# Decode attention with an MLP: four heads of wo moved to the end of the load stream, the final section inside the TensorE loop, wider value and weight products, and q with x stationary

## Chip, cores, metric

One core of a Trainium2 chip (trn2) runs the kernel. The metric is the device time of one execution in microseconds. Runs of this one-core program mostly agreed within 0.5% on one chip; a ratio is taken against runs of the kernel before on the same chip, in the same rounds.

## The reference

```python
x = A_x                                   # (4, 1, 448): four sequences, one token each
xn = layernorm(x)
q  = (xn @ wq)                            # 16 heads of 256; 8 K/V heads, so 2 q heads share one
s  = softmax(q k^T / 16) v  @ wo          # k, v caches: (4, 8, 8192, 256) bf16, 268 MB together
h  = layernorm(xn) @ w3; b = xn + gelu(h) @ w4      # at sequence length 1 the shift branch is zero
out = x + s * silu(b)
```

268 of the 279 MB read are K and V cache, and every byte is used once. There are 32 "heads" in the kernel's loop: 4 sequences times 8 K/V heads, each 4 MB of K and 4 MB of V.

## The kernel before

One DMA queue, issued by SyncE, carries all loads in one order. K and V have two buffers each; a load waits until its buffer is free, which for K is when the last transpose of the head before the last was copied out.

```python
# prog_sp: the load stream
wq -> vb[1];  w3, w4 -> vb[0];  load_k(0);  load_k(1)
wo (all 16 heads, one transfer)
for h in range(2, NH):
    load_k(h)            # waits for v_k >= h-1
    load_v(h - 2)        # waits for v_v
load_v(NH - 2)
load_v(NH - 1)           # the last V in four pieces: 2, 1, 0.5, 0.5 MB
```

TensorE transposes K in 128 by 128 blocks (DVE and ScalarE copy them out), forms scores, multiplies p by V two heads later, and at the end multiplies by wo.

```python
# prog_pe
... q product:   112 matmuls, wq stationary (128x128), xnT moving (8 columns)
... w3 product:  49 matmuls;   w4 product: 56 matmuls, 112 columns each, in four column groups
take(pe, "v_bout")
with nc.Fori(0, NH // 2, head_slot={PE: 0}):      # two heads a pass
    body(0); body(1)
h = NH - 1                                         # the final section follows the loop
f_bc(h); f_tr(h - 2); f_o(0..4); f_sum(h); f_pv(h - 1); f_o(5); f_tr(h - 1); f_o(6)
for i in range(4):                                 # the four V pieces of the last head
    take(pe, "dvl%d" % i, 16)
    ... 128 matmuls in all, V stationary
take(pe, "v_ot"); f_o(7)                           # 16 wo matmuls after the last V piece
# cut: body(h): 16 x (8 transposes, 8 score matmuls), and 64 value matmuls of 256 columns
```

## Time and profile before

| | before |
|---|---|
| time, median of three (range) | 661.82 us (660.87 to 663.16) |
| span of the profiled run | 658.7 us |
| read from HBM | 278.99 MB; 432 GB/s in the middle |
| one 4 MB load | 9.71 us of stream; a head needs two, 19.4 us |
| TensorE, one head, data ready, granted clock 1.00 | 14.13 us |
| last landing; out_b ready | 654.15 us; 656.59 us |

Three things have to be read here. The first is that the stream is the bound: one head takes TensorE 14.13 us and the stream 19.4.

The second is the start. Timeline of the kernel before, TensorE and SyncE (start us, us, engine, line, operation, out<-in, count, and in brackets how long the engine had been idle and what ended that):

```profile
21.77 1.48 PE L515 MATMUL pst<-vb,hT 128*4 128x112 bf16 x56 [1.88 <-PEq L219]
30.96 1.86 PE L528 MATMUL pst<-ident_b,kn 128*128 128x128 bf16 x16 [7.72 <-PEq L219]
...
43.85 0.33 SPq L183 DMA_DIRECT2D kn<-in_A_k_cache_dram  x1
64.95 0.33 SPq L183 DMA_DIRECT2D kn<-in_A_k_cache_dram  x1
...
82.61 0.33 SPq L183 DMA_DIRECT2D kn<-in_A_k_cache_dram  x1
```

The w4 product (L515) ends at 23.3 us; the K transposes (L528) begin at 30.96, as K of head 0 has landed (30.83). TensorE has 7 us in hand. K of head 2 is issued at 43.85 us. At that time wq, w3, w4, K 0 and K 1 are loaded and wo (3.67 MB) is still coming, until 50.23 us. So wo is what bridges the time until TensorE has freed the first K buffer. The stream by stretches of 2 us (each line: stretch, its length, busy us and count of PE, PEld, DVE, ACT, POOL, then the granted TensorE clock, the DMA share and GB/s) does not stop at these places:

```profile
44.00:46.00 2.00, 0.18 (x8) 0.05 (x2) 0.48 (x1) 0.00 (x0) 0.00 (x0) 0.87 1.03 379
46.00:48.00 2.00, 2.00 (x38) 0.94 (x38) 0.00 (x0) 0.00 (x0) 0.00 (x0) 0.50 1.27 479
86.00:88.00 2.00, 1.95 (x35) 1.79 (x32) 1.68 (x5) 1.02 (x1) 0.19 (x1) 1.00 0.99 426
88.00:90.00 2.00, 2.00 (x49) 2.00 (x47) 1.19 (x4) 1.65 (x6) 0.00 (x0) 1.00 1.03 442
```

The third is the tail. Timeline of the kernel before, then its DMA view from 640 to 649 us:

```profile
654.29 0.59 PE L630 MATMUL pst<-pT,kn 128*128 128x32 bf16 x16 [0.62 <-PEq L219]
655.03 0.23 DVE L472 TENSOR_TENSOR OT<-pst,rz 128x2 bf16<-128x2 f32 x2 [6.84 <-DVEq L219]
655.40 0.55 PE L610 MATMUL pst<-wo_sb,OT 128*4 128x112 bf16 x16 [0.53 <-PEq L219]
656.00 0.28 DVE L476 TENSOR_TENSOR res<-pst,sg 128x112 f32<-128x112 f32 x1 [0.74 <-PE pst L610]
656.31 0.28 DVE L478 TENSOR_TENSOR out_b<-res,x 128x112 bf16<-128x112 f32 x1
```

```profile
DMA packets 357, 3.58 MB, mean 398 GB/s; under 512 B 43, under 2 KB 43, under 8 KB 101
q1 hardware_dynamic: 356, 3.56, 94.2%
q8 instruction: 1, 0.02, 0.7%
```

After the last V piece 2.44 us pass until out_b is ready: value matmuls, a DVE product, 16 wo matmuls, two DVE operations. And one packet of the DMA view is no data: 16 KB of instructions (started at 644.15 us, 1.07 us long; another at 651.46).

What that packet does is seen in the landings. Every load has 16 landings in the trace, as many as the page counts DMA engines, so each is read here as one engine's. How far each of the 16 landed behind the first (us), in the kernel before:

| load | first, us | the sixteen, behind the first |
|---|---|---|
| V of head 30 | 640.39 | 0.00 0.14 0.68 0.75 0.76 0.77 1.12 1.22 1.62 1.63 1.69 1.74 1.84 1.93 2.15 **2.37** |
| V of head 31, piece 0 | 645.29 | 0.00 0.14 0.68 0.73 0.74 0.77 1.10 1.20 1.60 1.63 1.68 1.73 1.84 1.93 2.15 **3.96** |
| piece 3 | 650.31 | 0.00 0.14 0.68 0.69 0.75 0.77 1.08 1.18 1.54 1.64 1.68 1.74 1.79 1.88 2.09 **3.84** |

Fifteen engines keep their distance to a hundredth or so. One falls back by 1.6 us between 640 and 649 us, where the instruction packet lies, and never makes it up. The kernel waits for all sixteen (the value matmuls of the last piece start at 654.29, behind the last landing at 654.15), so there, where the slowest engine is 1.75 us behind the fifteenth in place of 0.23, this is about 1.5 us at the end of the kernel.

### The profile page before, as it was taken

The page shows a single profiled execution, that of the slowest core. Times are in us where ns is not written, and L with a number is a line of the kernel's source. Part 1 is how long each engine was busy: PE and PEld are TensorE (multiplying, and loading weights), DVE is VectorE, ACT ScalarE, POOL GpSimd, SP SyncE. Part 2 cuts the span into 40 slices and gives each one's busy share as a digit, 9 for nine tenths or more (in the row PEclk, how much of TensorE's full clock was granted, in tenths as well). Part 3 has the DMA queues.
Part 4 walks back from the last instruction along what each step waited for, and adds up shares of the span by engine and source line. Part 5 has one row for each costly group of instructions (what it writes and reads, how often), then busy time and mean ns, then how long its engine had stood idle before and what let it go on. Part 6 is the DMA issues. An engine that isn't in the chain of part 4 may idle for free. (4 is left out here: it accounts for less than half of the span.)

```text
span 658.7 us, 25245 instructions
## 1 busy us (share of the span) xinstructions
PE 531.3 (81%) x11091; PEld 481.5 (73%) x11091; DVE 260.7 (40%) x585; ACT 252.6 (38%) x362; POOL 17.0 (3%) x76
## 2 busy tenths in 40 slices
PE   1489999896979879678887867987969698867895
PEld 1378888885969778577777756877858688866784
DVE  7234455242433424343433434442524343433440
ACT  1044444451434435234443423443524344423340
POOL 4000000000000000000000000000000000000000
PEclk9988799696797969798987979896979896978996
DMA  8999999999999999999999999999999999999995
GB/s 363 433 410 427 427 432 430 434 434 430 432 432 430 432 434 430 434 432 434 428 434 428 432 432 436 430 432 436 426 434 430 436 430 434 434 426 436 426 426 223
DMA packets 12324, 279.18 MB, mean 424 GB/s; under 512 B 1172, under 2 KB 3224, under 8 KB 3736
## 3 DMA queue, kind: packets, MB, share of 16 engines
q1 hardware_dynamic: 12288, 278.99, 98.9%
q8 instruction: 10, 0.16, 0.1%
q14 instruction: 2, 0.02, 0.0%
q10 hardware_dynamic: 24, 0.01, 0.0%
HBM read 278.99 MB, written 0.00 MB: 424 GB/s over the span
## 5 line engine op out<-in xcount | busy, mean ns | idle before, releaser
L528 PE MATMUL pst<-ident_b,kn 128*128 128x128 bf16 x4096 | 345.5, 238 | 101.2 <-PEq L219 99.7
L265 ACT ACTIVATE kT<-pst 128x1024 bf16<-128x1024 bf16 x224 | 229.4, 1024 | 361.7 <-ACTq L219 361.1
L528 PEld LDWEIGHTS pst<-ident_b,kn 128*128 128x128 bf16 x4096 | 277.6, 108 | 106.4 <-issue 105.8
L263 DVE COPY kT<-pst 128x1024 bf16<-128x1024 bf16 x288 | 197.8, 692 | 282.5 <-DVEq L219 282.3
L540 PE MATMUL psc<-qc,kT 128*128 128x2 bf16 x4096 | 179.2, 165 | 0.7 <-issue 0.7
L540 PEld LDWEIGHTS psc<-qc,kT 128*128 128x128 bf16 x4096 | 158.8, 98 | 22.8 <-issue 22.8
L566 PE MATMUL psv<-vb,pT 128*2 128x256 bf16 x2112 | 84.8, 284 | 2.5 <-issue 1.8
L566 PEld LDWEIGHTS psv<-vb,pT 128*2 128x2 bf16 x2112 | 39.8, 84 | 10.9 <-issue 2.8
L407 DVE TENSOR_REDUCE rmax<-psc 128x2 f32<-128x128 f32 x32 | 9.3, 292 | 49.4 <-DVEq L219 49.4
L576 PE MATMUL psv<-sel,po 128*128 128x2 f32 x136 | 25.1, 289 | 0.7 <-PEq L219 0.6
L576 PEld LDWEIGHTS psv<-sel,po 128*128 128x128 f32 x136 | 23.0, 237 | 0.9 <-issue 0.9
L284 ACT ACTIVATE pT<-psc,negb 128x64 bf16<-128x64 f32 x66 | 20.6, 332 | 5.2 <-ACTq L219 5.2
L412 DVE TENSOR_REDUCE gmax<-psm 2x1 f32<-2x128 f32 x32 | 8.9, 279 | 33.9 <-DVEq L219 33.9
L250 POOL COPY qc<-qT 128x4 bf16<-128x4 bf16 x32 | 5.9, 187 | 584.1 <-DVEq L430 574.5
L552 PEld LDWEIGHTS psm<-diag,ones_f 2*128 2x128 f32 x66 | 12.7, 239 | 6.0 <-issue 4.6
L552 PE MATMUL psm<-diag,ones_f 2*128 2x2 f32 x66 | 15.4, 301 | 1.1 <-PEq L219 0.9
L431 DVE COPY po<-psv 128x256 f32<-128x256 f32 x33 | 14.0, 425 | 4.8 <-DVEq L219 4.1
L284 ACT ACTIVATION_READ_ACCUMULATOR pT<-psc,negb 128x1 f32 x66 | 13.6, 206 | 0.0
L557 PE MATMUL psm<-rowsum,ones_f 128*128 128x2 f32 x66 | 12.4, 257 | 0.0
L486 PE MATMUL pst<-ident_b,xn_b 4*128 4x4 bf16 x14 | 0.6, 161 | 13.5 <-DVE xn_b L333 8.8
L486 PEld LDWEIGHTS pst<-ident_b,xn_b 4*128 4x128 bf16 x14 | 0.5, 100 | 13.6 <-POOL ident_f L243 8.8
L557 PEld LDWEIGHTS psm<-rowsum,ones_f 128*128 128x128 f32 x66 | 10.3, 196 | 0.2 <-issue 0.2
(77 smaller groups left out, 97.1 us busy)
## 6 DMA issues: line engine op xcount, KB each, us to landing
kn<-in_A_k_cache_dram SPq DMA_DIRECT2D x32, 4096.0 KB, 26.0
vb<-in_A_v_cache_dram SPq DMA_DIRECT2D x31, 4096.0 KB, 31.7
vb<-in_A_wq_dram SPq DMA_DIRECT2D x1, 3584.0 KB, 11.3
wo_sb<-in_A_wo_dram SPq DMA_DIRECT2D x1, 3584.0 KB, 46.9
vb<-in_B_w_dram SPq DMA_DIRECT2D x2, 1568.0 KB, 16.3
kn<-in_A_v_cache_dram SPq DMA_DIRECT2D x1, 2048.0 KB, 27.1
kn<-in_A_v_cache_dram SPq DMA_DIRECT2D x1, 1024.0 KB, 29.1
kn<-in_A_v_cache_dram SPq DMA_DIRECT2D x2, 512.0 KB, 30.2
```

Of the source, the lines that this page charges most:

```text
L263: engine.tensor_copy(dst, src).then_inc(S["v_ev"], 1)
L265: engine.activation(dst, src, ACT.Copy).then_inc(S["a_ev"], 1)
L284: ins = act.activation(pv_p[:, :, hh], sc[:, :, hh], ACT.Exp, bias=negb[:, s, hh:hh + 1], scale=SCALE, accum_out=rowsum[:, s, hh:hh + 1])
L407: v.tensor_reduce(rmax[:, :], psc[h % 2][:, 0:NCH * REP].rearrange("p (k h) -> p h k", h=REP), AX.X, ALU.max).then_inc(S["v_rmax"], 1)
L412: v.tensor_reduce(gmax[:, :], psm[0:REP, 0:P], AX.X, ALU.max).then_inc(S["v_s"], 1)
L431: v.tensor_copy(po[:, :], psv[:, 0:DH]).then_inc(S["v_po"], 1)
L528: ins = pe.transpose(dst[:, t * P:(t + 1) * P], kn[:, h % 2, GC * j + kl, half * P:(half + 1) * P], ident_b[:, :])
L540: ins = pe.matmul(psc[h % 2][:, kk * REP:(kk + 1) * REP], kT[:, j % RING, t * P:(t + 1) * P], qc[:, h % 2, half, :], start=(half == 0), st ...
L552: pe.matmul(psm[:, P:P + REP], ones_f[0:REP, :], diag[:, :], start=True, stop=True).then_inc(S["p_m2"], 1)
L557: pe.matmul(psm[:, P + REP:P + 2 * REP], ones_f[:, :], rowsum[:, h % 2, :], start=True, stop=True).then_inc(S["p_m3"], 1)
L566: ins = pe.matmul(psv[o:o + REP, 0:DH], pT[:, h % 2, kk * REP:(kk + 1) * REP], vb[:, h % 2, kk, :], start=(kk < NCG), stop=(kk >= NCH - NCG))
L576: ins = pe.matmul(psv[:, o:o + REP], po[:, dh:DH:NHALF], sel[:, :], start=True, stop=True)
```

## The change

Its intent: load the last four heads' worth of wo behind the last V, so that little work is left after the last landing; keep instruction fetches out of the tail; make TensorE's code shorter. In parts:

1. wo is loaded in two portions: heads 4 to 15 early, heads 0 to 3 in three transfers at the very end.
2. The final section moves into the TensorE loop, under a condition, as a seventeenth pass.
3. Value matmuls take two K/V chunks at once (512 columns, half as many), and the turned sums, which fold the partial sums and bring d to the partitions, therefore take two tiles (four fp32 matmuls for two).
4. The q product has xn stationary (28 matmuls of 512 columns, then four transposes); the w4 product is 14 matmuls of 448 columns in place of 56 of 112, and its follow-up on DVE changes.
5. GpSimd makes the identities first; heads are taken from the last sequence to the first.

```diff
@@ prog_sp
-            sp.dma_start(wo_sb (all heads), A_wo ...).then_inc(S["dwo"], 16)
+            load_wo(NLATE, HQ, "dwo")
...
             load_v(NH - 1)
+            for i, hs in enumerate(LATE):                 # ((0, 1), (2,), (3,))
+                load_wo(hs[0], hs[-1] + 1, "dwl%d" % i)
@@ prog_pe, ahead of the loop
-            for c in range(NQC):
-                for j in range(DK):
-                    ins = pe.matmul(qo[:, g, hh, dh], wq_sb[:, j, c * P:(c + 1) * P], xnT[:, j], ...)
+            pe.wait_ge(S["g_c"], NPC)
+            for j in range(DK):
+                for i in range(NQD):
+                    ins = pe.matmul(q_ps[i * PQ:i * PQ + NHF * Bn, 0:QW], xnT[:, j] ..., 
+                                    wq_sb[:, j, i * QW:(i + 1) * QW], ...)
...
-                    for i in range(NQD):
-                        ins = pe.matmul(h2_ps[i * PQ:i * PQ + Bn, 0:DQ], hT[:, k, a, :],
-                                        w4_sb[:, a, k, i * DQ:(i + 1) * DQ], ...)
+                    ins = pe.matmul(h2_ps[0:Bn, 0:D], hT[:, k, a, :], w4_sb[:, a, k, :], ...)
@@ body and final section
-                for kk in range(lo, hi):
-                    ins = pe.matmul(psv[o:o + REP, 0:DH], pT[... REP columns], vb[:, h % 2, kk, :], ...)
+                for kk in range(lo, hi, CP):              # CP = 2
+                    ins = pe.matmul(psv[o:o + CP * REP, 0:CP * DH], pT[... CP * REP columns],
+                                    src[:, kk:kk + CP, :] ..., ...)
...
-            with nc.Fori(0, NH // 2, engines=[PE], head_slot={PE: 0}):
-                body(0)
-                body(1)
-            (final section)
+            with nc.Fori(0, NH // 2 + 1, engines=[e], head_slot={e: 48}) as it:
+                with pe.If(it != NH // 2):
+                    body(0)
+                    body(1)
+                with pe.If(it == NH // 2):
+                    finish()
# cut: DVE and GpSimd parts, buffers and semaphores that follow from these
```

## The prediction

> **What bounds it.** The load stream. The DMA view from 100 to 600 us shows all 16 engines at 99% or more and 432 GB/s. The landing records of the 4 MB loads come every 9.71 us from 57 us to 643 us without a gap. TensorE is not the bound: with data ready, one head takes 14.13 us at full clock (K issues at 82.61, 96.75, 110.88 us), against 19.4 us of stream; it idles 99.7 us before K transposes (waits view).
>
> **The tail.** V of the last head lands in four pieces, the last at 654.15 us. Then the timeline shows 16 value matmuls (0.59 us), a DVE product, 16 wo matmuls (0.55), two DVE operations (0.6), out_b ready at 656.59: 2.44 us, then the store. In the last 4 MB load before, the sixteenth DMA engine lands 0.22 us after the fifteenth; in the four pieces 1.75 to 1.8 us after. The DMA views for 640 to 649 and 649 to 655 us each show one 16 KB "instruction" packet (1.07 us each), and the rate fades from 430 to 27 GB/s, one engine's share, between 650 and 653.75. So TensorE's code after the loop is fetched by one of the engines that carry the data. [...]
>
> **What changes.**
> 1. Final code in the loop: it is fetched on the first pass, so the straggler should vanish from the tail: the last landing comes 1.5 us earlier.
> 2. Four heads of wo (0.92 MB, 2.4 us at the 378 GB/s of the wo transfer) last: bytes unchanged, but after the last landing stand 8 wo matmuls (0.3) and two DVE operations (0.6): about 1.1 us in place of 2.44. Gain 1.3 us if TensorE keeps up.
> 3. Cost of 2: the early stream has 2.4 us less cover. K of heads 2 and 3 is issued at 43.85 and 64.95 us, about 2.9 and 1.2 us before the least-lagging engines run dry. The third issue may leave a gap of 1 us, more if first-pass fetch stalls (1.8 and 1.5 us) fall worse. Loss 0 to 1.3 us, 0.4 expected.
> 4. Turned sums: 4 fp32 matmuls in place of 2, +0.6 us per head (0.61 us for the old two); value matmuls half as many at twice the width: same streaming. About +0.3 us per head, hidden in TensorE's slack, but in the tail at half clock the longer work may be late: 0.4 us expected, up to 2.
> 5. q with x stationary: before K 0 lands (30.83 us; TensorE idle 24 to 30.9). Worth nothing.
>
> Sum: 1.5 + 1.3 - 0.4 - 0.4 = 2.0 us. Predicted 659.8 us, range 658.0 to 662.0; faster by over 2%: 0.01, within 2%: 0.98, slower: 0.01.
>
> **Right if** no instruction packet lies in the last 20 us; the last landing trails the fifteenth by under 0.5 us and comes near 653; out_b follows it by 1 to 1.5 us; the chain of waits ends in wo matmuls; the middle keeps 432 GB/s and 9.71 us per load. **Wrong if** [...] TensorE at half clock is late in the tail (no wait before the last wo matmuls), or the stream shows a gap near 45 or 66 us.

The cuts take out what no trace of before shows (details of the instruction fetch, and a limit on the loop's length). The sum came to 2.0 us.

## The result

The kernel after took 661.94 us (661.43 to 662.34, four runs); before, in the same rounds, 661.35 (660.71 to 663.16). The ratio is 1.0004, 95% interval 0.9982 to 1.0026: the same. Ratios here are the mean time of one kernel's fast runs over that of the other's of the same rounds, so not quite the ratio of the medians. On a second chip it was 661.83 against 661.82, ratio 0.9992 (0.9964 to 1.0021). The expected 2 us are not there, though the profile shows that the tail got shorter. (One profile stands for each kernel here; e14 below is a second one of after, and its tail is longer.)

| | before | after |
|---|---|---|
| span, profiled run | 658.7 | 659.9 |
| K transposes begin | 30.96 | 32.47 |
| K of head 2 issued | 43.85 | 46.01 |
| K of head 4 issued | 82.61 | 86.90 |
| V of head 30 landed | 642.76 | 643.96 |
| last landing | 654.15 | 656.23 |
| last engine behind the fifteenth, last landing | 1.75 | 0.38 |
| out_b ready | 656.59 | 657.38 |
| 16 KB instruction packets, all / after 630 us | 10 / 2 | 7 / 0 |

The tail did what it should. Timeline of the kernel after, and its DMA view from 636 to 657 us, which has no instruction packet:

```profile
654.46 0.56 PE L684 MATMUL pst<-pT,kn 128*128 128x32 bf16 x16
655.16 0.18 DVE L516 TENSOR_TENSOR OT<-pst,rz 128x4 bf16<-128x4 f32 x1 [1.79 <-DVEq L242]
655.25 0.95 PE L674 MATMUL pst<-wo_sb,OT 128*32 128x112 bf16 x40 [0.24 <-PEq L242]
656.37 0.38 PE L674 MATMUL pst<-wo_sb,OT 128*32 128x112 bf16 x8 [0.17 <-PEq L242]
656.79 0.27 DVE L522 TENSOR_TENSOR res<-pst,sg 128x112 f32<-128x112 f32 x1 [1.45 <-PE pst L674]
657.10 0.28 DVE L524 TENSOR_TENSOR out_b<-res,x 128x112 bf16<-128x112 f32 x1
```

```profile
DMA packets 1233, 7.77 MB, mean 370 GB/s; under 512 B 128, under 2 KB 640, under 8 KB 896
q1 hardware_dynamic: 1233, 7.77, 89.3%
```

From the last landing (656.23) to out_b (657.38) it is 1.15 us, 1.29 less than before. What is lost was lost at the start. Timeline of the kernel after:

```profile
2.14 5.38 DVE L368 CAST x_f<-x_sb 4x448 f32<-4x448 bf16 x1 [0.73 <-DMA x_sb<-in_A_x_dram]
...
25.40 5.39 PE L564 MATMUL pst<-vb,hT 128*4 128x448 bf16 x14 [2.10 <-PEq L242]
32.47 1.05 PE L576 MATMUL pst<-ident_b,kn 128*128 128x128 bf16 x16 [1.68 <-PEq L242]
46.01 0.33 SPq L200 DMA_DIRECT2D kn<-in_A_k_cache_dram  x1
...
72.84 1.86 PE L576 MATMUL pst<-ident_b,kn 128*128 128x128 bf16 x16 [3.82 <-PEq L242]
86.90 0.33 SPq L200 DMA_DIRECT2D kn<-in_A_k_cache_dram  x1
```

and its stream in the four stretches that were shown for before:

```profile
44.00:46.00 2.00, 1.22 (x33) 1.12 (x29) 0.75 (x2) 0.73 (x1) 0.00 (x0) 1.00 0.75 267
46.00:48.00 2.00, 2.00 (x42) 1.07 (x42) 0.63 (x1) 0.00 (x0) 0.00 (x0) 1.00 0.90 254
86.00:88.00 2.00, 2.00 (x51) 1.49 (x48) 1.34 (x2) 0.53 (x1) 0.00 (x0) 1.00 0.63 197
88.00:90.00 2.00, 2.00 (x36) 0.76 (x34) 0.29 (x1) 0.00 (x0) 0.00 (x0) 1.00 0.88 311
```

In place of 379, 479, 426 and 442 GB/s there are 267, 254, 197 and 311. The stream ran dry twice, ahead of K of head 2 and ahead of K of head 4, because SyncE could not issue those loads: TensorE had not freed the buffers.

The loss can be added up from landings. wo's early transfer got shorter by 2.41 us (its first landing came at 45.38 in place of 47.79), so all later loads should land 2.41 us earlier. K of head 2 landed at 59.41 (59.95 before): 1.9 us lost. K of head 4 landed at 99.60 (98.79): 3.2 us lost. V of head 30 landed at 643.96 (642.76): 3.6 us lost. From there to the last landing before had 11.39 us; after has 9.95 to the last V piece, 1.44 less, for want of the straggler, and then 2.32 for the late wo. Together +1.20 - 1.44 + 2.32 = +2.08 us at the last landing, -1.29 after it: +0.79 at out_b. The spans differ by 1.2; the other 0.4 lies behind the landing of the store, and was not looked into.

### The profile page after: what moved, and what is told of

It reads as the page before. It is cut to its first block, busy times and chain, and to the rows that moved or that the text cites. A ratio compares the mean times of both kernels' runs of the same rounds, so it can differ in the third digit from the quotient of the medians.

```text
span 659.9 us, 22901 instructions
## 1 busy us (share of the span) xinstructions
PE 555.1 (84%) x9933; PEld 474.7 (72%) x9933; DVE 279.5 (42%) x592; ACT 251.4 (38%) x362; POOL 18.6 (3%) x79
## 5 line engine op out<-in xcount | busy, mean ns | idle before, releaser
L632 PE MATMUL psv<-vb,pT 128*4 128x512 bf16 x1056 | 87.3, 385 | 1.1 <-PEq L242 1.1
L606 PE MATMUL psm<-sel,po 128*128 128x2 f32 x272 | 36.6, 257 | 0.0
L606 PEld LDWEIGHTS psm<-sel,po 128*128 128x128 f32 x272 | 34.7, 196 | 0.0
L632 PEld LDWEIGHTS psv<-vb,pT 128*4 128x4 bf16 x1056 | 21.9, 82 | 16.6 <-issue 2.3
L468 DVE COPY po<-psv 128x512 f32<-128x512 f32 x34 | 23.5, 692 | 4.6 <-DVEq L242 3.9
L600 PEld LDWEIGHTS psm<-diag,ones_f 2*128 2x128 f32 x66 | 14.1, 265 | 6.5 <-issue 5.6
L600 PE MATMUL psm<-diag,ones_f 2*128 2x2 f32 x66 | 16.9, 323 | 1.1 <-PEq L242 0.9
L532 PE MATMUL pst<-ident_b,xn_b 4*128 4x4 bf16 x14 | 0.6, 161 | 16.6 <-DVE xn_b L362 11.9
L596 PEld LDWEIGHTS psm<-ident_f,rmax 128*2 128x2 f32 x32 | 2.6, 80 | 14.3 <-issue 14.3
L532 PEld LDWEIGHTS pst<-ident_b,xn_b 4*128 4x128 bf16 x14 | 0.5, 100 | 16.6 <-issue 11.9
```

Source lines behind the costliest of these rows:

```text
L468: v.tensor_copy(po[:, slot], psv[:, 0:CP * DH]).then_inc(S["v_po"], 1)
L600: pe.matmul(psm[:, P:P + REP], ones_f[0:REP, :], diag[:, :], start=True, stop=True).then_inc(S["p_m2"], 1)
L606: ins = pe.matmul(dst(dh)[:, 0:width], po[:, slot, i * DH + dh:(i + 1) * DH:NHALF], sel[:, i, 0:width], start=(i == 0), stop=(i == CP - 1))
L632: ins = pe.matmul(psv[o:o + CP * REP, 0:CP * DH], pT[:, h % 2, kk * REP:(kk + CP) * REP], src[:, kk:kk + CP, :].rearrange("p c d -> p (c d)"),
```

## The experiments

Twelve kernels ran. Theory 1: the gain was spent in gaps of the early stream, because TensorE reaches the loop late and is held up again at the first back edge. Theory 2: the late wo transfers are slow in themselves. A second pair came up later: theory A, short code keeps fetches out of the tail and the place in the loop only costs; theory B, the place in the loop is what keeps them out. Times in us; "issue" is when SyncE issued that K; "gap" is read from landings.

| run | built on | time (range) | ratio to before (95%) | K 2 issue | K 4 issue | last landing | out_b |
|---|---|---|---|---|---|---|---|
| after | | 661.94 (661.43 to 662.34) | 1.0004 (0.9982 to 1.0026) | 46.01 | 86.90 | 656.23 | 657.38 |
| e1 | after, narrow w4 | 662.27 (660.13 to 664.91) | 1.0017 (0.9997 to 1.0037) | 47.58 | 88.06 | 658.37 | 660.22 |
| e2 | after, memsets wait | 660.27 (659.89 to 662.33) | 0.9995 (0.9979 to 1.0012) | 44.78 | 85.36 | 656.01 | 657.82 |
| e3 | after, final section outside | 660.54 (659.78 to 660.66) | 1.0002 (0.9985 to 1.0019) | 44.98 | 79.88 | 653.66 | 654.71 |
| e4 | after, wo all early | 661.25 (659.85 to 663.78) | 1.0018 (0.9990 to 1.0045) | 44.76 | 84.95 | 652.58 | 656.70 |
| e5 | before, final section inside | 853.12 (845.82 to 860.42) | two runs | | | | |
| e8 | e3, head slot 239 | 664.14 (661.49 to 666.11) | 1.0056 (1.0012 to 1.0100) | 47.94 | 79.77 | 656.48 | 658.17 |
| e9 | e3, narrow w4, slot 110 | 659.78 (658.44 to 662.86) | 0.9995 (0.9953 to 1.0036) | 44.27 | 78.52 | 653.85 | 654.99 |
| e10 | e9, memsets last | 658.90 (658.48 to 659.76) | 0.9970 (0.9942 to 0.9999) | 44.54 | 79.52 | 653.21 | 655.02 |
| e14 | after again | 661.83 (660.92 to 664.64) | 0.9992 (0.9964 to 1.0021) | 45.12 | 88.26 | 656.96 | 660.07 |
| e15 | e10 again | 659.56 (658.80 to 660.50) | 0.9958 (0.9930 to 0.9987) | 44.49 | 78.99 | 653.20 | 654.97 |
| e13 | e10, final section inside | 661.47 (660.60 to 664.04) | 0.9993 (0.9962 to 1.0024) | 45.82 | 87.44 | 655.94 | 657.08 |
| e12 | e10, slot 239 | 659.55 (659.31 to 659.79) | 0.9960 (0.9914 to 1.0006) | 44.41 | 76.23 | 652.88 | 654.65 |

e1 to e4 ran on one chip, each beside its own runs of before. Landings and issues come from the one profiled run of each, which is one draw from the range: e1's, e2's, e10's and e14's profiles fell on their slowest run, e3's and e12's on their fastest.

**e1: the w4 product in its old form.**

```diff
-                    ins = pe.matmul(h2_ps[0:Bn, 0:D], hT[:, k, a, :], w4_sb[:, a, k, :], ...)
+                    for i in range(NQD):
+                        ins = pe.matmul(h2_ps[i * PQ:i * PQ + Bn, 0:DQ], hT[:, k, a, :],
+                                        w4_sb[:, a, k, i * DQ:(i + 1) * DQ], ...)
 # and DVE's bout, sg, x4, xn4 as in before
```

> The kernel after, with the product with w4 taken back to the form of before (56 matmuls over four column groups in place of 14 wide ones; DVE code of it as before). Theory 1, the gain was lost in gaps of the early load stream, because TensorE reaches the loop late (first K transposes at 32.47 us, K of head 2 issued at 46.01): transposes start at about 30.6, that issue comes at about 44.2, the landing of K of head 2 about 1.8 us earlier than 59.41, the last landing at 653 to 654 in place of 656.23, time 658.5 to 659.8. Theory 2, the late wo loads are slow by themselves and put 2.3 us behind the last V piece: last landing stays at 656 and the time at 661.9, whatever TensorE does at the start.

A miss: no gain. The product became short, but the transposes did not start earlier. Timeline of e1:

```profile
25.38 1.48 PE L565 MATMUL pst<-vb,hT 128*4 128x112 bf16 x56 [1.89 <-PEq L242]
32.60 1.65 PE L578 MATMUL pst<-ident_b,kn 128*128 128x128 bf16 x14 [5.75 <-PEq L242]
```

The w4 product ended at 26.9 us, K 0 had landed at 29.6, and TensorE still stood idle until 32.60. A 16 KB instruction packet lies at 29.8 us, inside that wait. The 42 extra matmuls (each is two instructions: the trace has a weight load for every matmul) had, it seemed, made the prologue (the code ahead of the loop) so long that the loop head came only with one more packet; in after the packets lie at 26.06 and 42.56 us, with none between. That became theory 1b, tested in e9, where another head slot was to move that packet.

**e2: GpSimd's large memsets wait for DVE's cast of x.**

```diff
+            gp.wait_ge(S["v_c"], 2)
             c(gp.memset(vflat[1][:, DK * HDH:NCH * DH], 0.0))
             c(gp.memset(vflat[0][:, DK * FH + NF * D:NCH * DH], 0.0))
```

> The kernel after, with the two large GpSimd memsets of vb made to wait until DVE's cast of x is done. The cast took 5.38 us in after (1.29 in before) and ended as the second memset ended. Theory 1: the cast falls to under 0.5 us, the q product starts about 3.4 us earlier, the w4 product ends by about 27.5 to 28, transposes start on the landing of K 0 at 30.6 and the rest is as in e1 (last landing 653 to 654, time 658.5 to 659.8). If the cast stays slow, the memset is not what slowed it. Theory 2: time stays at 661.9.

The cast is as expected, the rest is not. Timeline of e2:

```profile
3.28 0.38 DVE L369 CAST x_f<-x_sb 4x448 f32<-4x448 bf16 x1 [1.88 <-DMA x_sb<-in_A_x_dram]
...
5.91 3.10 DVE L353 TENSOR_SCALAR xn_f<-x_f,st 4x448 f32<-4x448 f32 x1
```

0.38 us in place of 5.38: it was the memsets that held DVE (by what means, no trace shows). But the clash only moved: the second memset now ran from 5.47 to 8.77 us, and DVE's next product, the TENSOR_SCALAR above, took 3.10 us beside it in place of 0.50 in after. TensorE's first transposes, which need what follows from it, began at 11.46 in place of 11.94, and the w4 product at 24.89, only 0.5 us earlier. Its time is no verdict on theory 1.

**e3: the final section behind the loop.**

```diff
-            with nc.Fori(0, NH // 2 + 1, engines=[e], head_slot={e: 48}) as it:
-                with pe.If(it != NH // 2): body(0); body(1)
-                with pe.If(it == NH // 2): finish()
+            with nc.Fori(0, NH // 2, engines=[e], head_slot={e: 48}):
+                body(0); body(1)
+            finish()
```

> The kernel after, with the final section behind the loop again, as in before. Theory 1: the 3.8 us stop of TensorE at the first back edge (69.0 to 72.8 us) goes, K of head 4 is issued near 83 in place of 86.90 and its landing loses the 1.3 us gap; but one or two 16 KB instruction packets come back in the last 20 us and the last engine lands 1.4 us or more after the fifteenth. The two cancel: last landing 655.5 to 656.5, time within 0.7 us of 661.9. Theory 2: no gap near 87 us matters, so only the straggler is added: last landing near 657.7, time near 663.3.

Half of it holds, and the other half fell in the kernel's favour. The stop at the back edge went, and K of head 4 was issued at 79.88. But no instruction packet came back in the tail: the last engine trails by 0.08 us, and the last landing is at 653.66, 2.6 us earlier than in after. So the loop is not needed to keep the straggler away. (Whether it keeps fetches away is another question, see under e13.) The time shows little of it: spans were 657.2 to 658.6 us against 657.9 to 658.8 of before on that chip, and the ratio is 1.0002. That single-part answer came clearer in e13 and e15.

**e4: all of wo early.**

```diff
             load_wo(NLATE, HQ, "dwo")
+            for i, hs in enumerate(LATE):
+                load_wo(hs[0], hs[-1] + 1, "dwl%d" % i)
 ...
-            for i, hs in enumerate(LATE):
-                load_wo(hs[0], hs[-1] + 1, "dwl%d" % i)
```

> The kernel after, with the three late wo loads issued right behind the first wo load at the start, all else the same. Theory 1: the early stream gets back 2.4 us of cover, the gap before K of head 2 shrinks from 1.9 us to under 0.3, a gap of 1 to 1.5 us stays before K of head 4; last landing (now a V piece) near 654, out_b 2.2 to 2.5 us behind it; time 660.5 to 661.5. Theory 2: no gaps are at play, the 2.3 us of wo leave the end of the stream and come back at its start, so out_b only loses the shorter tail: about 1.2 us slower than after, 663.

With 2.4 us of cover given back, K of head 2 landed at 59.4 and V of head 30 at 642.71 (before: 59.95 and 642.76), although TensorE was no faster than in the other kernels with the final section in the loop (K 4 issued at 84.95). There is no net loss in the early stream any more, less even than expected. So the gaps in after are the price of moving wo: theory 1, and theory 2 falls, since the same late transfers cost 2.3 us in both places. The tail missed the expectation the other way: out_b came 4.1 us after the last landing in place of 2.2 to 2.5, as TensorE was slow and behind (its 48 wo matmuls took 1.48 us from 654.59 us on, as long as in e10 at a granted clock of 0.50).

**e5: before, with only the final section moved into the loop.**

```diff
-            with nc.Fori(0, NH // 2, engines=[PE], head_slot={PE: 0}):
-                body(0); body(1)
-            (final section)
+            with nc.Fori(0, NH // 2 + 1, engines=[e], head_slot={e: 48}) as it:
+                with pe.If(it != NH // 2): body(0); body(1)
+                with pe.If(it == NH // 2): finish()
```

> The kernel before with one part of the change alone: its final section put into the TensorE loop under a condition, nothing made smaller. Theory A, the short code is what frees the tail of fetches, the place in the loop is not: by the matmul count (two instructions each) the loop is then about 2000 instructions [...] so TensorE fetches again in every pass: over 40 instruction packets of 16 KB, one engine late in every load, time 670 us or more. Theory B, being in the loop is what frees the tail: no instruction packet after 80 us, last engine within 0.5 us of the fifteenth, last landing near 652.7 us, time about 1.5 us below before, less what a stop at the first back edge costs.

Theory A, and by more than expected: 853 us. (Its two runs differ by 1.7%; the fast one, 845.82 us, is still 28% above before.) Page of e5, its stream in 40 slices and its queues, and under them the same queue in before and after:

```profile
GB/s 390 406 426 425 247 434 135 414 373 268 419 196 423 272 416 372 176 430 208 436 328 352 422 187 432 209 436 327 289 417 204 418 250 390 398 285 422 109 368 4
q8 instruction: 148, 2.42, 1.2%
```

```profile
q8 instruction: 10, 0.16, 0.1%
```

```profile
q8 instruction: 7, 0.11, 0.1%
```

148 instruction packets in place of 10 (before, from which e5 differs in TensorE's code alone) and 7, and a stream that falls to 109 to 250 GB/s again and again. Counting two instructions for each matmul, and an fp32 matmul twice as the trace records it, the loop of e5 has about 1,980 instructions and some waits and branches; that of after, with the same parts, about 1,590. Both lengths are estimates, and at what length between them the fetches begin to return in every pass was not shown; 148 packets over 17 passes are 8.7 a pass, where after has none behind 78 us. So it is the shorter code, halved value matmuls above all, that makes the place in the loop possible at all. It is no gain by that.

**e8: e3 with another slot for the loop head.** The edit is `head_slot={e: 48}` to `head_slot={e: 239}`.

> e3_outside (final section behind the loop) with one number changed: [...] Theory A (fetches in the tail make one DMA engine late[...]): one or two 16 KB instruction packets come back between 635 and 656 us, the last engine lands 0.8 to 1.8 us after the fifteenth, last landing 0.8 to 1.8 us later than the 653.66 of e3. Rival (the straggler of before comes from the four V pieces or from load order, not from fetches): tail as in e3, spread 0.1 us.

Inconclusive for its question. How far the new slot moves the code, and in which direction, no trace shows. One packet came in the tail, at 654.31 us. The landings don't show it (spread 0.08), but TensorE does: it stood still for 1.32 us, until 656.76, ahead of the late wo matmuls, whose first load had landed at 655.36, and out_b came 1.69 us after the last landing in place of 1.05 in e3. The first pass was hit too: TensorE stood still for 2.02 us until 41.8 us (packet at 39.3), K of head 2 was issued at 47.94, and the last landing moved by 2.8 us against e3. Another head slot alone was worth that much.

**e9: e3 with the old w4 product, and the loop head at slot 110, behind the longer prologue.**

> e3_outside with the w4 product of before (as in e1) and the loop head at slot 110[...]. In e1 the w4 product was done at 27 us, but the transposes started only at 32.6, after a 16 KB fetch at 29.8. Theory 1b: that fetch was for the loop head[...]. Then here no fetch lies between 27 and 31 us, transposes start at 30.4 to 30.8 (landing of K 0), K of head 2 is issued at 44.0 to 44.4, its landing is at 57.5 to 58.0 (58.5 in e3), last landing 652.7 to 653.4, time 0.5 to 1 us below e3. If transposes start at 32 or later without a fetch before them, theory 1b falls.

As expected at the start. Timeline of e9:

```profile
25.39 1.47 PE L565 MATMUL pst<-vb,hT 128*4 128x112 bf16 x56 [1.88 <-PEq L242]
30.53 1.87 PE L578 MATMUL pst<-ident_b,kn 128*128 128x128 bf16 x16 [3.67 <-PEq L242]
```

There is no instruction packet between 27 and 31 us (they are at 26.0 and 31.9; in e1 one is at 29.8), transposes begin at 30.53, on the landing of K 0, and K of head 2 landed at 57.6: nothing lost up to there. Theory 1b holds: with the slot moved, the packet left the wait. The last landing (653.85) missed 652.7 to 653.4, because one engine fell back by 1.0 us at about 70 us, where a packet lies (69.2), and stayed there to the end.

**e10: e9 with the memsets of vb at the end of GpSimd's list.**

```diff
             c(gp.memset(rz[:, :, :].rearrange("p s r -> p (s r)"), 1.0))
             assert c.n == NPC
+            gp.wait_ge(S["v_c"], 2)
+            (the two memsets of vb)
+            c.sync()
```

> e9 with the two large memsets of vb at the end of GpSimd's list, behind DVE's cast of x, and nothing waiting on them but the loop. The cast should take 0.4 us in place of 5, the q product start near 13.5 to 14.5 us in place of 17.2, the w4 product near 21.5 to 22.5. As K 0 bounds the start of the loop anyway, no more than 0.3 us over e9 is expected; if e9 fails to start at 30.8, this should.

The cast took 2.31 us, as smaller memsets still ran beside it (from 2.25 to 4.29 us); and, as in e2, the TENSOR_SCALAR behind it took 3.10 us beside the second memset. So the clash moved again and was not removed. The w4 product began at 24.98, a few tenths earlier; the expectation of 21.5 to 22.5 was missed, and as K 0 bounds the start it did not matter. Last landing 653.21, time 658.90, with a ratio to before just clear of 1. The landing is earlier than in e9 because no engine fell back here (the fifteenth engine landed at 653.15, in e9 at 652.89), not because of the memsets.

**e14, e15, e13, e12: after, the best version, and two single edits of it, on one chip.** e13 is e10 with the final section inside the loop; e12 is e10 with slot 239.

> The kernel after, unchanged, beside the next two on one chip. Its earlier four runs were 661.4 to 662.3 us. Expected 661 to 662.5 here, within 0.3% of before, TensorE idle 3.8 to 6.2 us at the first back edge.

> e10 unchanged (final section behind the loop, w4 product of before, memsets of vb last, loop head at slot 110), on the same chip as after and the next one. Expected 658.5 to 659.5 us, 1.5 us below before and 2 to 3 us below after.

> e10 with the final section put into the TensorE loop as in after, all else as in e10. Theory A (the place in the loop costs and gains nothing here, since the short code already keeps fetches out of the tail): TensorE stops 3.8 to 6.2 us at the first back edge near 66 to 70 us, K of head 4 is issued at 83 to 86 in place of 79.5, its landing may come up to 1 us late, the tail's spread between the engines stays as in e10; time 0.3 to 2 us above e10. Theory B (the place in the loop is what frees the tail): time at or below e10.

> e10 with the loop head at slot 239 in place of 110. [...] Theory A (a fetch in the tail makes one DMA engine late): a 16 KB instruction packet near 642 to 648 us, and the last engine trails the fifteenth by 0.6 to 1.2 us in all loads landing after it, while in the load before it trails as little as before. Rival: packet or not, the spread does not change.

After gave 661.83 and the best version 659.56; e13 gave 661.47. All six runs of e13 were slower than all six of e15. So the place in the loop costs about 1.9 us of time and gains none: theory A. First transposes of head 2 in after, e14, e13 and e15:

```profile
74.24 1.01 PE L576 MATMUL pst<-ident_b,kn 128*128 128x128 bf16 x8 [6.12 <-PEq L242]
```

```profile
73.92 1.33 PE L580 MATMUL pst<-ident_b,kn 128*128 128x128 bf16 x11 [5.21 <-PEq L242]
```

```profile
67.16 0.27 PE L600 MATMUL psm<-ident_f,rmax 128*2 128x128 f32 x1
67.27 1.05 PE L580 MATMUL pst<-ident_b,kn 128*128 128x128 bf16 x16
```

With the final section in the loop TensorE stands still for 6.12 and 5.21 us (3.82 in the first profile of after) at the first back edge; without it the transposes follow the last matmul of head 1 within 0.11 us. Each of those waits has a 16 KB packet in it (at 71.0, 70.8 and 69.6 us). The first pass jumps over the final section to the loop's end, and what stands there has, it seems, not been fetched yet. In all six profiles of the changed kernel with it inside, K of head 4 was issued between 84.95 and 88.26 us; in all six with it outside, between 76.23 and 79.88. K of head 4 of e13 landed at 99.5, of e15 at 97.0; 1.1 of these 2.6 us were lost ahead of the back edge, as K of head 2 landed at 59.18 and 58.06.

On fetches, though, theory B is the better one. None of the six profiles with the section inside (after, e1, e2, e4, e13, e14) has an instruction packet after 78 us. Of the six with it outside, five have one in the tail before out_b is ready: e12 at 644.49 and 653.02, e15 at 651.03, e9 at 651.17, e10 at 653.25, e8 at 654.31; only e3 has none. So short code does not by itself keep fetches out of the tail. It is that these packets did not make the last engine later: in e15 the last engine trails the fifteenth by 0.01 to 0.05 us before and after.

e12 puts the prediction's own mechanism to the test, and both theories have a share. The packet came in the stretch that theory A had named (642 to 648 us), where e15, with slot 110, has none before 651.03. DMA view of e12 from 641 to 647 us:

```profile
DMA packets 296, 2.43 MB, mean 405 GB/s; under 512 B 29, under 2 KB 29, under 8 KB 104
q8 instruction: 1, 0.02, 1.1%
```

It started at 644.49 us. Yet the last engine trails the fifteenth by 0.06 us after it, as before it. The sixteen landings show why:

| load of e12 | first, us | the sixteen, behind the first |
|---|---|---|
| V of head 31, piece 0 | 643.74 | 0.00 **0.01** 0.06 0.10 0.13 0.15 0.23 0.27 0.27 0.58 0.65 0.92 0.94 1.73 1.76 1.82 |
| piece 1 | 646.22 | 0.00 0.07 0.10 0.12 0.17 0.23 0.26 0.27 0.58 0.66 0.90 0.92 **1.52** 1.73 1.76 1.83 |

One engine of the first six (by the gaps between the others, most likely the one at 0.01) fell back by 1.4 to 1.5 us, much as one did in before. But here it had 1.8 us in hand over the slowest. In before the engine that fell back was the slowest already (2.37 us behind the first, the fifteenth 2.15). So a fetch in the tail can make one engine late, and then it costs stream time only if that engine is among the last; the expectation, that it always would, was wrong. The packets from 651 us on left no step in the landings at all, but one of them stopped TensorE (e8).

## Why the prediction was right or wrong

The measured time lies in the stated range and the class (within 2%) is right. The sum behind it was not: 2.0 us of gain were expected, and there was none. That the time lies in the range is luck: 661.94 is 0.06 below its upper end, and the range took in no change at all (before: 661.35 in the same rounds). Of the prediction's own signs for being right, the tail's came true (no packet, 0.38 behind the fifteenth, out_b 1.15 after the last landing), but the last landing was not near 653 (656.23); and one of its signs for being wrong came true, the gap near 45 us.

- *What bounds it* held. From 110 us on loads land every 9.71 us in before and 9.72 in after; over 55 loads that is the last 0.4 us of the loss below.
- *Step 1, the straggler, 1.5 us:* measured 1.44. The reason given, "Final code in the loop", does keep fetches out of the tail (six profiles of six with a loop of about 1,590 instructions or less; e5 has it inside with about 1,980, and 148 packets). But it was not needed for the 1.44 us: e3 and e15 have the code outside and no straggler. When a packet comes and which engine it hits decide whether it costs (e12), and the head slot (651.03 us in e15, 644.49 and 653.02 in e12) and the length of the code (29.8 in e1, where after has none from 26.06 to 42.56) move it. How much of this is the shorter code alone is not shown: before was not run with just another head slot.
- *Step 2, the shorter end, 1.3 us:* measured 1.29 in the profile of after (2.44 to 1.15), but it varied with the granted clock, see step 4.
- *Step 3, "Loss 0 to 1.3 us, 0.4 expected":* this is the term that failed. The loss was 3.6 us. The cover of wo was counted rightly (2.4 us), but two things set against it were not. First, the time in hand: K of head 2 was said to be issued 2.9 us before the stream runs dry. Where the stream had run dry, the first engine landed 11.6 to 11.9 us after the issue (K of head 4 in after: 86.90 to 98.64), which is 9.71 of stream and about 2.0 more. So in before, with the issue at 43.85 and wo's first landing at 47.79, only 1.9 us were in hand. With 2.41 less cover and an issue 2.16 us later (46.01), an estimate of the gap on the first engine is 2.6 us, and that is what it was (57.72 where 55.10 would be no loss; 1.9 by the last engine). Second, TensorE's lateness was taken as that of before. It began 1.5 us later, it took 14.91 us a head in place of 14.13 (issues at 86.90 and 101.81), which was foreseen as +0.3 and measured +0.78, and it stood still for 3.82 us at the first back edge, which was not foreseen at all.
- *Step 4, turned sums late in the tail, 0.4:* in the first profile of after TensorE was in time, at a granted clock of 0.78 from 650 to 655 us (before: 0.50). The wider value matmuls were busy 87.3 us in all, the old ones 84.8. TensorE waited 0.24 and 0.17 us ahead of the last wo matmuls. At a granted clock of 0.50 (e10 from 648 us on) it was late, and the wo matmuls ran through without a wait for data. So in e15, whose wo matmuls took the same 1.48 us. Timeline of e15:

```profile
652.86 1.48 PE L678 MATMUL pst<-wo_sb,OT 128*32 128x112 bf16 x48
```

There out_b came 1.77 us after the last landing, and in e1, e2, e10 and e12 1.77 to 1.85. In e14, the same kernel as after, it was 3.11: TensorE ran at 0.50 from 646 to 656 us and fell behind, so that the tail gained nothing. The mean over the eleven profiles with the late wo is 1.66, 0.8 us less than the 2.44 of before; steps 2 and 4 together had forecast 0.9.
- *Step 5, "Worth nothing":* it was worth less than nothing. DVE's cast of x took 5.38 us in place of 1.29, so the q product began at 17.2 in place of 14.1; and the w4 product took 5.39 us in place of 1.48, at a granted clock of 0.50, which is 385 ns for each of the 14. The old form's 56 matmuls of 112 columns are the same 6,272 columns and took 1.48 us at a granted clock of 1.00: 3.6 times less, where the granted clocks differ by 2. That its four column groups overlapped is the estimate from these figures, not tested. The 7 us in hand were used up and 1.5 more.

As for the gain: 1.44 + 1.29 us came, and 3.6 went, 1.9 ahead of K of head 2 and most of the rest ahead of K of head 4. Undoing the place in the loop and the wide w4 product, with a head slot to fit, brought most of it back (moving the memsets had little to do with it): e15 loses 0.6 us in the early stream (V of head 30 at 640.99, where 640.35 would be no loss), lands last at 653.20, and is 0.42% faster than before (0.13% to 0.70%).

What stays open: whether the late wo is worth it in the best version (it was undone only in after, in e4, where the time is not told apart from after's); whether before would have lost its straggler with another head slot alone; why the wait at the first back edge varies between 3.8 and 6.2 us; and the spread of 660 to 666 us that before had on the last chip. That the waits at the first back edge are instruction fetches is inferred from the packets inside them.

## What to carry to other kernels

In a kernel bound by its load stream, a load moved from the start to the end takes away cover that bridges the time until the first buffers come free: before moving it, read when those loads are issued and by how much the stream has work left, with the compute as it will be, not as it was. Count instructions: here a loop of about 1,980 had 148 instruction packets of 16 KB and took 28% more time (e5's fast run), one of about 1,590 had 7 (after), and another head slot moved the end of the stream by 2.8 us (e8). Code that runs once did better behind the loop than in it under a condition here, by 1.9 us (e13, e15), although one fetch then fell in the tail. A DVE cast of 0.38 us took 5.38 beside two GpSimd memsets (e2, after): look for such pairs at the start. And read the tail in more than one profile: the same kernel had out_b 1.15 and 3.11 us after the last landing.
